# Attention with a top-32 mask and a gated product on one core: where GpSimd's difference of g, x's rounding and the copies of scores stand in their queues

## The chip, the cores and the metric

The kernel runs on one core of a Trainium2 chip. The time is the device time of one execution in microseconds, as the median of several runs. The engines of the core are TensorE (PE, with its weight loads PEld), VectorE (DVE), ScalarE (ACT), GpSimd (POOL) and SyncE (SP, which issues the DMAs). Each works through its own queue in order and waits on semaphores of the others.

## What is computed

For 8 batches and 8 heads of 576 rows and 64 columns, each row of scores keeps its 32 largest, goes through a softmax and multiplies v. The joined heads (4608 x 512) then go through three products:

```python
scores = scale * np.matmul(q, k.transpose(0, 1, 3, 2))
kth = np.partition(scores, -32, axis=-1)[..., -32:-31]
scores = np.where(scores >= kth, scores, -1e9)
attn = softmax(scores)
x = np.matmul(attn, v).transpose(0, 2, 1, 3).reshape(B * S, H * D)
out = ((x @ w1) * (x @ w2)) @ w3 @ w_out
```

## The kernel before

The attention is cut into 144 slots. A slot is 128 rows of two heads, 128 x 2 x 576 scores, found at lines 31 to 34 and listed at line 461. Twelve slots give 384 rows of x, one MoE block (`BLOCK`, line 38). w3 and w_out are multiplied together once at the start, into `wf`. To keep the precision of 32-bit numbers in rounded matmuls, x, g and the weights are each held as a rounded part and the difference to it, and a product takes three matmuls.

The main loop (line 568) has one step `p` per slot, and works on several slots at different stages at once: i = p + 1 has its scores copied from PSUM to SBUF, slot p is searched for its 32 largest, j = p - 1 is masked and goes through the exponential, l = p - 2 is normalised, and m = p - 3 is turned (transposed) and multiplied with v. All engines keep the order in which the program issues (`InOrder`, line 50), so where a line stands in the loop is where its instruction stands in the engine's queue.

In one step, the names and lines that matter here:

- ACT: `take_scores` (248) copies the scores of slot i in two parts: part 0 are columns 0 to 383 out of a bank pair called wide, part 1 columns 384 to 575 out of the tile `rest`. Even and odd slots have different wide banks (wide0, wide1) and share `rest` (`scores_whole`, 228). Then come the Relus of `mask` (295), evictions of MoE results, the copies of the turned weights (`take_turned`, 339), `normalise`, and the exponentials (`exps`). At the end of the loop body `split_high` (367) rounds x.
- DVE: `top32_steps` (255) folds the 576 columns in four instructions (`w<-s` twice, `w<-w,s` twice) and then takes four rounds of eight maxima with replacements between. `split_low` (370) follows the fold and takes the difference of x, `invert` the reciprocal, and `take_b` (377) the product of a and b.
- POOL: `edges_of` (272) makes `edge` (and `over`) from the maxima, `add_up` the sums, `mask` subtracts the Relu twice (`pab<-s,pab`; the first waits for the fold of the next slot), and `take_b` the difference of g.
- PE: `turn` (321) makes ten transposes, one of them into `rest`, eight into wide0, in each step. In even steps the scores of two slots and the values (`values`, 345) of two slots follow.

The MoE block is a generator (`moe_steps`, 373) that issues one matmul at each call, and `fill` (494) takes 12 of them at fixed places: one group of 12 in an even step, three in an odd one (`SHARES`, 46). A block begins in an odd step: 16 groups of 12 for a and b, two per f, then 8 groups for the four outputs. What follows a full group is put off until the next `evict`: a copy of a to `asb` on ACT (`take_a`), or `take_b`: the product with b on DVE, the rounding to g on ACT, and the difference on POOL. The outputs need rounded part and difference of all eight g.

`asb` and the output tile `osb` share two buffers; g has eight.

Of the kernel before, what the change touches and what calls it, by code (L numbers as in the profile page):

```python
# [9 lines left out]
F32 = mybir.dt.float32  # L10
# [4 lines left out]
ALU = mybir.AluOpType  # L15
# [55 lines left out]
def attn_moe(ctx: ExitStack, tc: tile.TileContext, q, k, v, w1, w2, w3, w_out, out, flag, any_missed, general):  # L71
    nc = tc.nc
    pe, act, dve, pool, sp = nc.tensor, nc.scalar, nc.vector, nc.gpsimd, nc.sync
# [37 lines left out]
    if not general:  # L111
        pe, act, dve, pool, sp = (InOrder(tc, e) for e in (pe, act, dve, pool, sp))
# [132 lines left out]
    def new_s():  # L245
        return att_p.tile([128, 2, S], F32, tag="s", name="s", bufs=S_BUFS)

    def take_scores(s, st, h):
        if isinstance(st[h], tuple):
            src, lo, hi = st[h]  # L250
        else:
            src, (lo, hi) = st[h][:, :, :HS], HALVES[h]
        act.copy(s[:, :, lo:hi], src)
# [41 lines left out]
    def mask(s, edge, pab, a, after=None):  # L295
        act.activation(pab[:, a, :], s[:, a, :], AF.Relu, bias=edge[:, a, 1:2], scale=-STEEP)
        ins = pool.tensor_tensor(pab[:, a, :], s[:, a, :], pab[:, a, :], op=ALU.subtract)
        if after is not None:
            tc.add_manual_dep(
                ins.ins, after.ins.name, mybir.DependencyInfo(mybir.DependencyClass.Sync, mybir.DependencyReason.DATA),  # L300
                reason="the fold of the next slot goes before the masking",
            )
# [64 lines left out]
    def split_high(high, low, whole):  # L367
        act.copy(high, whole)

    def split_low(high, low, whole):  # L370
        dve.tensor_tensor(low, whole, high.bitcast(F32), op=ALU.subtract)

    def moe_steps(xs, nb, places, after):
        def take_a(p, asb):
            act.copy(asb[:, :nb], p[:, :nb])

        def take_b(p, asb, gf):
            whole = asb[:, :nb]
            dve.tensor_tensor(whole, p[:, :nb], whole, op=ALU.mult)
            act.copy(gf[:, 0, :nb], whole)  # L380
            pool.tensor_tensor(gf[:, 1, :nb], whole, gf[:, 0, :nb].bitcast(F32), op=ALU.subtract)

        def take_o(p, e):
            osb = o_p.tile([128, NB], F32, tag="o", name="osb")
            act.copy(osb[:, :nb], p[:, :nb])
            for place, cut in places:
                sp.dma_start(place(slice(e * 128, (e + 1) * 128)), osb[:, cut])

        g = []
        for f in range(NFC):  # L390
            asb = o_p.tile([128, NB], F32, tag="o", name="asb")
            g.append(late["g"].tile([128, 2, NB], F32R, tag="g", name="g"))
            for i in range(2):
                p = late["mm"].tile([128, 512], F32, tag="mm", name="ab")
                for c in range(NCC):
                    for n, (w, x) in enumerate(((wh, 0), (wh, 1), (wl, 0))):
                        pe.matmul(
                            p[:, :nb], w[i][:, c * DF + f * 128 : c * DF + (f + 1) * 128], xs[c][:, x, :nb],
                            start=(c == 0 and n == 0), stop=(c == NCC - 1 and n == 2),
                        )  # L400
                        if (c, n) != (NCC - 1, 2):
                            yield
                if i == 0:
                    after(lambda p=p, asb=asb: take_a(p, asb))
                else:
                    after(lambda p=p, asb=asb, gf=g[f]: take_b(p, asb, gf))
                yield
        for e in range(NEC):
            p = late["mm"].tile([128, 512], F32, tag="mm", name="eo")
            for f in range(NFC):  # L410
                for n, (i, j) in enumerate(((0, 0), (1, 0), (0, 1))):
                    pe.matmul(
                        p[:, :nb], wf[i][:, f * DM + e * 128 : f * DM + (e + 1) * 128], g[f][:, j, :nb],
                        start=(f == 0 and n == 0), stop=(f == NFC - 1 and n == 2),
                    )
                    if (f, n) != (NFC - 1, 2):
                        yield
            after(lambda p=p, e=e: take_o(p, e))
            yield
# [82 lines left out]
    def begin():  # L502
        while starting:
            while going or fetched or waiting:
                warm()
            if not late:
                settle()
            n = starting.pop(0)
            queue.append(moe_steps([xs[n, hp] for hp in range(NHP)], NB, places[n], put_off.append))
# [24 lines left out]
    def warm():  # L534
        entered.append(p)
        if p < 0:
            return
        if fetched and len(entered) % 2 == 0:
            z, step = fetched.pop(0)
            going.append(step(z))  # L540
        going[:] = [unit for unit in going if next(unit, "end") != "end"]
        prefetch(WAITING)
# [20 lines left out]
    def scored(h):  # L563
        renew(kts, load_k, h)
        if h + 1 == n_slots or group_of[h + 1] != group_of[h]:
            renew_q(group_of[h] + 2)

    for p in range(-2, n_slots + 4):
        h, i, j, l, m = p + 2, p + 1, p - 1, p - 2, p - 3
        if p == 1:  # L570
            vts[0, 0] = load_v(0, 0)
            vts[0, 1] = load_v(0, 1)
            vts[0, 2] = load_v(0, 2)
            vts[0, 3] = load_v(0, 3)
        finder = top32_steps(ss[p], p) if 0 <= p < n_slots else iter(())
        if 0 <= i < n_slots:
            ss[i] = new_s()
            take_scores(ss[i], sts[i], 0)
            take_scores(ss[i], sts[i], 1)
        if 0 <= j < n_slots:  # L580
            edges[j] = edges_of(j)
        if 0 <= l < n_slots:
            add_up(pabs[l][1])
        folded = next(finder, None)
        for part in fresh:
            split_low(*part)
        fresh.clear()
        warm()
        if 0 <= j < n_slots:
            pabs[j] = new_weights()  # L590
            for a in range(2):
                mask(ss[j], edges[j], pabs[j][0], a, folded if a == 0 else None)
        warm()
        begin()
        fill(SHARES[p % 2][0])
        evict()
        next(finder, None)
        if 0 <= m < n_slots:
            turned[m] = take_turned(pabs[m][0], *turn(pabs[m][0], None if ("wide", 0) in late else sts[i][1]))
        if 0 <= l < n_slots:  # L600
            invert(pabs[l][1])
            normalise(*pabs[l])
        if 0 <= j < n_slots:
            exps(edges[j], *pabs[j], 0)
        warm()
        if p == 3:
            stir(6)
        fill(SHARES[p % 2][1])
        next(finder, None)
        warm()  # L610
        if h not in sts and (not late or h % 2) and h < n_slots:
            score(h, scores)
            scored(h)
        elif h % 2 == 0:
            for n in (h + 1, h):
                if n < n_slots:
                    score(n, lambda *a, n=n: scores_whole(*a, n % 2))
            for n in (h, h + 1):
                if n < n_slots:
                    scored(n)  # L620
            homes[:] = [wide_banks(1)[:, a, SPLIT:] for a in range(2)]
        if 0 <= j < n_slots:
            exps(edges[j], *pabs[j], 1)
        if 0 <= m < n_slots:
            if not put_back(m):
                for n in [m - 1, m] if put_back(m - 1) else [m]:
                    b, hps, t = slots[n]
                    ovs[n] = values(of(vts, b), hps, *turned.pop(n), n < m)
                    renew(vts, load_v, n)
        if p == 14:  # L630
            stir(9)
        next(finder, None)
        warm()
        fill(SHARES[p % 2][2])
        for _ in finder:
            pass
        for d in sorted(ovs):
            b, hps, t = slots[d]
            n = d // BLOCK
            for hp in hps:  # L640
                if (n, hp) not in xs:
                    xs[n, hp] = new_x(n)
            fresh += parts_of([xs[n, hp] for hp in hps], column[group_of[d]], t, ovs.pop(d))
            del ss[d], pabs[d], edges[d], sts[d]
            if (d + 1) % BLOCK == 0:
                starting.append(n)
        for part in fresh:
            split_high(*part)
        if p == 2:
            stir(8)  # L650
        warm()
    begin()
    worst = small.tile([128, B + 1], F32, tag="worst", name="worst", bufs=1)
    dve.tensor_reduce(worst[:, 1:], over[:].rearrange("p (b i) -> p b i", b=B), axis=AX.X, op=ALU.max)
# [65 lines left out]
```

## Time and profile before

| | us |
|---|---|
| time, median of 3 runs (1315.67 to 1315.72) | 1315.68 |
| the profiled execution, its own time | 1318.25 |
| its span, first to last instruction | 1316.5 |
| DVE busy | 1192.0 |
| PE busy | 1197.6 |
| ACT busy | 1112.7 |
| POOL busy | 777.4 |

The first 190 us bring in and unpack the weights beside the first slots; from there to about 1235 us the steady part runs; the last 50 us are the last MoE block, on PE almost alone. In the rows below a line of the timeline gives the start and the length in us, the engine, the instruction with the tile that it writes and those that it reads, and in brackets the idle time of the engine before it and what ended it. Instructions that follow at once are merged (x2). The ends of matmuls are modelled.

### The profile page before, as it was taken

The numbers are of one execution on the slowest core, as the hardware profiler recorded it, in microseconds if no ns is written. First come the engines' busy times: TensorE is split into PE (matmuls) and PEld (weight loads), VectorE is DVE, ScalarE is ACT, GpSimd is POOL, SyncE is SP. The second block draws the span as 40 slices with busy tenths as digits, with TensorE's granted clock in tenths as the row PEclk, the third lists the DMA queues.
The fourth block names the chain that finished last, engine by engine and source line by source line (L and its number), as shares of the span: only waits on it lengthen the run. The fifth ranks groups of instructions, "written<-read, shape, count | busy, mean of one in ns | idle before, by whom it ended". The sixth has DMA issues, their size and how long they took to land.

```text
span 1316.5 us, 27368 instructions
## 1 busy us (share of the span) xinstructions
PE 1197.6 (91%) x9427; PEld 1039.0 (79%) x9427; DVE 1192.0 (91%) x3952; ACT 1112.7 (85%) x2233; POOL 777.4 (59%) x877
## 2 busy tenths in 40 slices
PE   5788689999999999999999999999999999999998
PEld 3444368888888888888888888888888888888998
DVE  7999999999999999999999999999999999999710
ACT  5988989989989989989989989989989989889821
POOL 4778766656656656656656656656656656656511
PEclk6899899999999999999999999999999999999999
DMA  7334210100120020101120020101120020100000
GB/s 283 113 120 153 96 57 9 60 27 30 35 71 9 16 75 9 60 28 30 35 71 9 15 75 9 60 28 31 34 70 10 15 76 9 60 27 1 13 13 26
DMA packets 30117, 64.73 MB, mean 49 GB/s; under 512 B 5396, under 2 KB 11540, under 8 KB 29972
## 3 DMA queue, kind: packets, MB, share of 16 engines
q1 hardware_dynamic: 29972, 62.93, 14.7%
q8 instruction: 75, 1.23, 0.4%
q14 instruction: 70, 0.57, 0.1%
HBM read 53.48 MB, written 9.44 MB: 48 GB/s over the span
## 4 chain that ended last, share of the span: by engine, by line
PE 49%; ACT 26%; DVE 14%; issue 6%; POOL 4%; DMA 1%; SPq 0%; ACTq 0%; POOLq 0%; DVEq 0%
PE wide L60 22%; ACT pab L60 18%; PE ab L60 14%; PE eo L60 7%; DVE w L60 5%; PE rest L60 5%; ACT s L60 5%; DVE top L60 5%; POOL pab L60 2%; DVE t L60 1%; POOL g L60 1%; ACT g L60 1%; DVE x L60 1%; DMA z<-in_wo 1%; ACT x L60 1%
## 5 line engine op out<-in xcount | busy, mean ns | idle before, releaser
L60 POOL TENSOR_TENSOR pab<-s,pab 128x576 f32<-128x576 f32 x288 | 404.8, 1428 | 145.9 <-PE ab L60 49.2
L60 DVE MAX8 top<-w 128x8 f32<-128x192 f32 (+1 forms) x1152 | 465.7, 445 | 0.0
L60 PE MATMUL ab<-x,wh 128*128 128x384 f32 x1536 | 408.0, 347 | 0.6 <-ACT asb L60 0.5
L60 DVE MATCH_REPLACE8 w<-top,w 128x192 f32<-128x192 f32 x864 | 289.3, 342 | 0.0
L60 PEld LDWEIGHTS ab<-x,wh 128*128 128x128 f32 x1536 | 271.1, 188 | 8.7 <-issue 7.3
L60 PE MATMUL ab<-x,wl 128*128 128x384 f32 x768 | 259.7, 338 | 0.0
L60 POOL TENSOR_TENSOR g<-asb,g 128x384 fp32r<-128x384 f32 x96 | 105.5, 1099 | 252.9 <-ACT g L60 252.9
L60 ACT ACTIVATE pab<-s,edge 128x576 f32<-128x576 f32 x288 | 210.5, 789 | 37.4 <-POOL edge L60 37.4
L60 ACT ACTIVATE pab<-pab,edge 128x576 f32<-128x576 f32 x288 | 220.6, 774 | 1.2 <-POOL pab L60 1.2
L60 PE MATMUL eo<-g,wf 128*128 128x384 f32 x1152 | 220.0, 344 | 0.0
L60 ACT ACTIVATE pab<-pab,sums 128x576 f32<-128x576 f32 x288 | 209.7, 785 | 10.2 <-DVE sums L60 10.2
L60 DVE TENSOR_TENSOR w<-s 128x384 f32<-128x384 f32 x288 | 193.2, 711 | 14.8 <-ACT s L60 7.6
L60 PEld LDWEIGHTS eo<-g,wf 128*128 128x128 f32 x1152 | 199.8, 188 | 3.4 <-issue 3.1
L60 DVE TENSOR_TENSOR w<-w,s 128x384 f32<-128x384 f32 x288 | 168.3, 584 | 4.9
L60 PE MATMUL wide<-pab,vt 128*64 128x128 f32 (+1 forms) x2960 | 160.1, 264 | 0.6 <-ACT pab L60 0.6
L60 PEld LDWEIGHTS wide<-pab,vt 128*64 128x64 f32 x2960 | 144.7, 137 | 16.1 <-issue 15.3
L60 PE MATMUL wide<-ident,pab 128*128 128x128 f32 x1040 | 152.2, 272 | 0.0
L60 ACT COPY pab<-wide 128x1024 f32<-128x1024 f32 x130 | 132.1, 1016 | 17.6 <-PE wide L60 12.9
L60 PEld LDWEIGHTS ab<-x,wl 128*128 128x128 f32 x768 | 144.2, 188 | 0.0
L60 PEld LDWEIGHTS wide<-ident,pab 128*128 128x128 f32 x1040 | 125.6, 140 | 4.5
L60 POOL TENSOR_TENSOR edge<-top,coef 128x4 f32<-128x4 f32 x144 | 72.8, 505 | 67.3 <-DVE top L60 67.2
L60 PE MATMUL wide<-kt,qt 64*128 64x384 f32 (+1 forms) x560 | 108.6, 506 | 0.7 <-ACT pab L60 0.7
(64 smaller groups left out, 1394.9 us busy)
## 6 DMA issues: line engine op xcount, KB each, us to landing
z<-in_w SPq DMA_DIRECT2D x32, 512.0 KB, 3.6
vt<-in_v SPq DMA_DIRECT2D x32, 352.0 KB, 4.4
qt<-in_q SPq DMA_DIRECT2D x40, 256.0 KB, 2.8
kt<-in_k SPq DMA_DIRECT2D x32, 320.0 KB, 3.4
out_t<-osb SPq DMA_DIRECT2D x32, 192.0 KB, 1.9
z<-in_wo SPq DMA_DIRECT2D x8, 512.0 KB, 8.2
out_t<-osb SPq DMA_DIRECT2D x16, 160.0 KB, 1.8
out_t<-osb SPq DMA_DIRECT2D x16, 32.0 KB, 1.6
```

Source lines behind the costliest of these rows:

```text
L60: ins = fn(*args, **kw)
```

## The change

Three things are put elsewhere; no instruction is added or taken away. POOL's difference of g is no longer issued in `take_b` but kept in a list, and issued in the main loop behind the masks of the next step. ACT copies part 1 of the scores (from `rest`) ahead of part 0. The rounding of x moves from the end of the loop body to the next step, behind its copies of scores.

```diff
+    lows, behind_masks = [], []
+
+    def take_lows():
+        while lows:
+            lows.pop(0)()
+
     def moe_steps(xs, nb, places, after):
...
-            pool.tensor_tensor(gf[:, 1, :nb], whole, gf[:, 0, :nb].bitcast(F32), op=ALU.subtract)
+            lows.append(lambda: pool.tensor_tensor(gf[:, 1, :nb], whole, gf[:, 0, :nb].bitcast(F32), op=ALU.subtract))
+            if not behind_masks:
+                take_lows()
...
+    behind_masks.append(True)
     for p in range(-2, n_slots + 4):
...
             ss[i] = new_s()
+            take_scores(ss[i], sts[i], 1)
             take_scores(ss[i], sts[i], 0)
-            take_scores(ss[i], sts[i], 1)
+        for part in fresh:
+            split_high(*part)
         if 0 <= j < n_slots:
             edges[j] = edges_of(j)
...
                 mask(ss[j], edges[j], pabs[j][0], a, folded if a == 0 else None)
+        take_lows()
         warm()
         begin()
...
-        for part in fresh:
-            split_high(*part)
         if p == 2:
             stir(8)
         warm()
+    take_lows()
+    behind_masks.clear()
     begin()
```

## Rows read from the trace of the kernel before

**Rows 1.** The page, part 1: busy us, share of the span, instructions.
```profile
PE 1197.6 (91%) x9427; PEld 1039.0 (79%) x9427; DVE 1192.0 (91%) x3952; ACT 1112.7 (85%) x2233; POOL 777.4 (59%) x877
```

**Rows 2.** One block: busy PE, PEld, DVE, ACT, POOL; granted clock, DMA share, GB/s.
```profile
587.38:685.79 98.41, 92.52 (x732) 82.99 (x732) 94.80 (x321) 87.42 (x176) 59.01 (x69) 1.00 0.16 45
```

**Rows 3.** Waits, whole span: us in total, times, longest.
```profile
PE rest L60 <- ACT s L60: 61.5, 63, 1.2
```

**Rows 4.** The chain that ended last, two of its pieces in the steady part.
```profile
602.91 1.08 ACT s L60 x2
...
604.04 0.33 PE rest L60
```

**Rows 5.** Timeline of PE.
```profile
548.63 3.60 PE L60 MATMUL eo<-g,wf 128*128 128x384 f32 x19
...
571.06 0.33 PE L60 MATMUL rest<-ident,pab 128*128 128x128 f32 x1 [1.24 <-ACT s L60]
...
604.04 0.33 PE L60 MATMUL rest<-ident,pab 128*128 128x128 f32 x1 [0.98 <-ACT s L60]
...
620.61 0.33 PE L60 MATMUL rest<-ident,pab 128*128 128x128 f32 x1 [0.98 <-ACT s L60]
```

**Rows 6.** Timeline of ACT.
```profile
578.47 0.43 ACT L60 CAST x<-wide 128x128 fp32r<-128x128 f32 x2 [1.84 <-PE wide L60]
...
602.41 0.50 ACT L60 CAST g<-asb 128x384 fp32r<-128x384 f32 x1
602.81 0.80 ACT L60 COPY s<-wide 128x768 f32<-128x768 f32 x1
603.50 0.48 ACT L60 COPY s<-rest 128x384 f32<-128x384 f32 x1
604.82 1.45 ACT L60 ACTIVATE pab<-s,edge 128x576 f32<-128x576 f32 x2 [0.83 <-POOL edge L60]
...
611.70 0.43 ACT L60 CAST x<-wide 128x128 fp32r<-128x128 f32 x2 [0.75 <-PE wide L60]
...
615.04 1.02 ACT L60 COPY pab<-wide 128x1024 f32<-128x1024 f32 x1
...
618.97 0.50 ACT L60 CAST g<-asb 128x384 fp32r<-128x384 f32 x1
```

**Rows 7.** Groups of instructions by form, whole span: count, busy us, mean ns.
```profile
L60 DVE TENSOR_TENSOR w<-s 128x384 f32<-128x384 f32 x288 | 193.2, 711 | 14.8 <-ACT s L60 7.6
L60 POOL TENSOR_TENSOR g<-asb,g 128x384 fp32r<-128x384 f32 x96 | 105.5, 1099 | 252.9 <-ACT g L60 252.9
```

**Rows 8.** Timeline of DVE.
```profile
560.34 1.03 DVE L60 TENSOR_TENSOR w<-s 128x384 f32<-128x384 f32 x2
...
601.45 1.41 DVE L60 MAX8 top<-w 128x8 f32<-128x576 f32 x2
602.89 1.83 DVE L60 TENSOR_TENSOR w<-s 128x384 f32<-128x384 f32 x2
...
606.29 0.34 DVE L60 MATCH_REPLACE8 w<-top,w 128x192 f32<-128x192 f32 x1
...
609.03 0.34 DVE L60 MATCH_REPLACE8 w<-top,w 128x192 f32<-128x192 f32 x1
```

**Rows 9.** Timeline of POOL.
```profile
548.02 2.82 POOL L60 TENSOR_TENSOR pab<-s,pab 128x576 f32<-128x576 f32 x2 [0.86 <-ACT pab L60]
...
602.99 1.32 POOL L60 TENSOR_TENSOR g<-asb,g 128x384 fp32r<-128x384 f32 x1 [2.76 <-ACT g L60]
604.27 0.51 POOL L60 TENSOR_TENSOR edge<-top,coef 128x4 f32<-128x4 f32 x1
...
605.96 2.80 POOL L60 TENSOR_TENSOR pab<-s,pab 128x576 f32<-128x576 f32 x2
```

**Rows 10.** The chain in the start, two pieces one step apart.
```profile
93.15 2.20 ACT pab L60 x4
...
105.67 2.20 ACT pab L60 x4
```

## Prediction

> **What bounds the kernel now.** I read the page first: PE and DVE are each busy 91% of the span, ACT 85%, POOL 59% [rows 1]. No engine is full, so shares decide nothing and I went to the steady part. Work repeats every two steps (an even one that scores and multiplies by v for two slots, an odd one that does neither) and every six such pairs (one MoE block). One block lasts 98.4 us at the full granted clock (1.00, the 2.4 GHz level), of which DVE is busy 94.8, PE 92.5 and ACT 87.4 [rows 2]. Next the waits: PE waits 63 times, 61.5 us in all, for a copy of scores by ACT before the transpose that goes into the shared bank `rest`; once per even step, 0.98 us each [rows 3]. Then the chain: in the steady part it runs PE's transpose into `rest`, the 12 MoE matmuls, the scores, the 40 value matmuls, ACT's rounding of x, ACT's odd step, g's rounding, two copies of scores, and the same transpose again [rows 4]. DVE appears there only for short stretches.
>
> One pair in numbers, from the two transposes into `rest` at 604.04 and 620.61 [rows 5]: 7.66 us until ACT rounds x at 611.70, 3.34 until ACT may copy the turned weights at 615.04 (that is PE's odd group and its turning, not ACT), 3.93 of ACT work to g's rounding at 618.97, and 1.64 for g's rounding, both score copies and the hand-over [rows 5, 6]. Sum 16.57. This loop is the bound.
>
> **Part 1, the shared bank's scores first.** In an even step ACT rounds g at 602.41, copies the wide scores at 602.81 and the `rest` scores at 603.50; the latter ends at 603.98 and PE's transpose goes at 604.04 [rows 5, 6]. So PE follows the `rest` copy by 0.06 us. With it first, it starts at 602.81 and PE goes 0.69 us (603.50 - 602.81) earlier. ACT's own work stays the same, and the wide copy then lies beside PE's transposes, whose bank (wide0) it doesn't read in an even step (it reads wide1, needed again only by the scores over 2 us later). Of PE's 0.98 us wait 0.29 is left, so PE doesn't become the limit before the whole 0.69 is taken. 63 waits x 0.69 = **43.5 us**. In odd steps nobody waits for the order. The fold on DVE reads scores copied one step before, so it doesn't notice.
>
> **Part 2, x's rounding behind the copies.** Today it stands ahead of the odd step's score copies, where ACT waits 0.75 us for the values with 1.06 us of copies (0.69 and 0.37) queued behind [rows 6]. After the edit the copies fill that wait. But ACT's turned copy at 615.04 waits for PE anyway, so this shortens nothing in the loop: x, the two Relus and a's copy take 0.33 + 1.34 + 0.36 = 2.0 us of the 3.34. The gain is slack, and odd masks that can start earlier. Its price is an x up to 0.2 us later, hidden by the same slack. DVE's difference of x comes behind its fold in any case, and the first MoE group of a new block needs x only in its later matmuls. Taken as 0, bounds -0.3 to +0.3 per block.
>
> **Part 3, g's difference behind the masks.** It removes no instruction: 96 subtractions of 1.10 us [rows 7] move past edge, over, sums and both masks. Two effects.
> First, DVE. With a g subtraction beside it the first half of the fold takes 1.83 us (602.89, subtraction at 602.99); in steps without one it takes 1.03 (560.34) [rows 8, 9]. The mean over all 288 instructions is 0.711 against 0.515 in the free step: 288 x 0.196 = 56 us, some 5 us of DVE per block [rows 7, 8]. So DVE's need falls from 94.8 to about 90. This is needed: at the shorter block of 93.7 to 94 us 94.8 wouldn't fit.
> The Trainium skill has a rule that speaks against the new place: SBUF — State Buffer, section "SBUF: two separate sides", says that a VectorE instruction with two SBUF inputs and a GpSimd instruction that reads SBUF lock each other out whole. By it the replacements behind the masks, which read both `w` and `top`, could be caught. The trace does not show that: a replacement takes 0.34 us beside the masks (606.29) and 0.34 after them (609.03) [rows 8]. Were they caught, it would be the first rival below, with the price that stands there.
> Second, the edge. It stands behind the subtraction on POOL: at 604.27 though top was ready at 602.86, so the Relus wait 0.83 us [rows 6, 8, 9]. In such pairs the copy of the turned rest comes late and PE's scores wait: 7.66 us from transpose to x instead of 7.41 (571.06 to 578.47) [rows 5, 6]. I count two such pairs per block, 0.25 to 0.33 each. Without the subtraction ahead, edge would be ready by 602.86 + 0.05 + 0.51 = 603.4, before the Relu can follow the copies at about 603.9 [rows 6, 8, 9]. 0.6 x 10.5 blocks = **6 us**.
>
> The wait it adds: the subtraction waits for nothing new (g's rounding is done), and behind it on POOL is only the next edge, some 2 us later. What waits for it is PE: the twelfth matmul of the second output group of a block reads the last g's difference. That group starts at 548.63 with 0.18 us per matmul, so its last goes at about 550.7; the masks of that step run 548.02 to 550.84 and the moved subtraction would end at 551.8 [rows 5, 9]. The masks waited 0.86 us for ACT's Relus there [rows 9], which come earlier after part 2; of that I count half, 0.4, because the fold holds the masks too. So PE waits about 0.7, of which 0.29 lies in what is left of its wait for ACT. Bounds 0 and 1.1 per block; I take 0.3: 11 x 0.3 = **3 us** lost. The buffers of a and of g, two and eight deep, come free a whole step before they are needed.
>
> **Start and end.** In the first 190 us a step takes 12.5 us in a loop of DVE and ACT (normalising at 93.15, 105.67) in which score copies don't stand [rows 10]. x's rounding changes places with the copies there at equal sum. Bounds -1 and +2 us, taken +0.5. The tail is PE's last MoE block, with the subtraction at once as before. Queues of DMAs issue what they did; no load moves past another.
>
> **Sum.** -43.5 - 6 + 3 + 0.5 = -46. The profiled execution has a span of 1316.5 and a time of 1318.25; the median of the runs is 1315.68, so I take the 46 from the median: **1269.5 us**. A block should take 93.8 instead of 98.4.
>
> **Rivals.**
> *DVE becomes the bound.* The subtraction finds DVE in the new place too, or the fold stays slow beside other POOL work. With no relief DVE needs 94.8 per block and more for its waits, 95.5; with every subtraction costing it a full microsecond (8 per block) 90 + 8 = 98. Saved are then 0.4 to 2.9 us of each of 10.5 blocks: 1285 to 1311, about 1297 in the middle. Against it: masks of 2.8 us already lie beside the same DVE work without lengthening it [rows 8, 9].
> *PE's transpose waits for both copies.* The row names ACT and s, not which copy. Then only the edge's 6 us come: about 1310; where the edge gives nothing either, 1315, no change. Against it: the start is 0.06 us behind the `rest` copy's end and 0.43 behind the wide copy's [rows 5, 6].
> *The last difference of g is late,* the one that would end slower. If POOL's masks slip at the start of the outputs, PE stands in its queue with everything behind it. Each microsecond beyond 0.29 costs 11 us; the gain of 49 is gone at 4.7 us. At 6 us it gives 1266 + 11 x 5.7 = 1329. Against it: the masks before that group waited 0.86 [rows 9].
> *More than forecast.* If the wait of PE goes entirely, because something ahead in ACT's chain shrinks too: 61.5 + 6 off, 1248. Against it: each piece of ACT's 3.93 us stays.
>
> **How the numbers follow.** Forecast 0.72, own range 1260 to 1280 (the bounds of the small terms). DVE bound 0.13, both copies 0.07 (half of it no change), last difference 0.03, more than forecast 0.05. For 8 in 10 the range runs from 1258 to 1288, which takes in the forecast and the near side of the first rival. About 0.2% is what a measurement of this kernel can tell from none. Faster 0.72 + 0.13 + 0.05 + 0.035 = 0.93, within 0.04, slower 0.03.
>
> **What would show it.** Right: PE's wait for ACT's s falls to about 0.3 us, 63 times (about 20 us in all); the distance of transposes into `rest` falls to about 15.6 us; the fold's first half takes 1.03 us in all steps and DVE's mean for it falls to near 0.52; the wait of ACT for edge is nearly gone; POOL's g stands behind pab. Wrong: PE's wait names another ACT row at equal length, or DVE shows no idle time, or PE's `eo` waits for POOL's g by more than a microsecond.

## The result and the profile after

The changed kernel takes 1271.55 us (median of 4 runs, 1270.52 to 1272.72), the kernel before 1315.70 on the same chip (1315.67 to 1317.92): a ratio of 0.9661, 95% interval 0.9644 to 0.9677, 44 us less. The profiled execution took 1270.52 us at a span of 1268.7, against 1318.25 and 1316.5 before.

The page, part 1, of the kernel after (busy us, share of the span, instructions), to be read against [rows 1]:

```profile
PE 1194.6 (94%) x9427; PEld 1036.4 (82%) x9427; DVE 1142.0 (90%) x3952; ACT 1108.1 (87%) x2233; POOL 769.8 (61%) x877
```

Every engine has the instructions it had. DVE is busy 50 us less, nearly all of it the fold (below); PE's and ACT's work is what it was, in a shorter span.

Two blocks of the kernel after by the table of windows (length; busy PE, PEld, DVE, ACT, POOL; granted clock, DMA share, GB/s); the second has the instruction counts of [rows 2]:

```profile
474.97:568.93 93.96, 92.56 (x828) 82.99 (x829) 90.56 (x325) 87.24 (x181) 58.30 (x69) 1.00 0.10 33
568.93:662.62 93.69, 92.17 (x732) 82.78 (x732) 90.28 (x321) 86.98 (x177) 58.28 (x69) 1.00 0.16 48
```

A block takes 93.69 us instead of 98.41, and DVE's work in it 90.28 instead of 94.80. The clock is the full one in both. Some 10.5 blocks of 4.7 us make 49 us, about the 47.8 by which the two spans differ.

The waits of the kernel after (total us, times, longest), over the whole span, which answer to [rows 3]:

```profile
PE rest L60 <- ACT s L60: 14.5, 53, 0.3
...
PEld eo L60 <- POOL g L60: 7.1, 11, 2.6
PE eo L60 <- POOL g L60: 3.4, 7, 2.3
```

PE's wait for the copies of scores has gone from 61.5 to 14.5 us. The wait of the outputs (`eo`) for the last difference of g is new, as the prediction feared, and small in all; but one of the seven waits of PE is 2.3 us long, and a wait of more than a microsecond there was one of the prediction's signs of being wrong. It is taken up below, at the run that issues the last g at once.

The chain that ended last in the kernel after, across one hand-over (start, length, what), against [rows 4], where two copies stood in one piece:

```profile
489.74 0.40 ACT g L60
490.14 0.38 ACT s L60
...
490.57 0.33 PE rest L60
```

One pair on the timeline of PE, of ACT and of POOL, as in [rows 5, 6, 9] (start and length in us, engine, instruction, idle time before it and its cause):

```profile
490.57 0.33 PE L60 MATMUL rest<-ident,pab 128*128 128x128 f32 x1 [0.28 <-ACT s L60]
...
506.21 0.33 PE L60 MATMUL rest<-ident,pab 128*128 128x128 f32 x1 [0.28 <-ACT s L60]
```
```profile
490.05 0.47 ACT L60 COPY s<-rest 128x384 f32<-128x384 f32 x1
490.42 0.80 ACT L60 COPY s<-wide 128x768 f32<-128x768 f32 x1
491.11 1.46 ACT L60 ACTIVATE pab<-s,edge 128x576 f32<-128x576 f32 x2
...
501.35 1.01 ACT L60 COPY pab<-wide 128x1024 f32<-128x1024 f32 x1 [0.56 <-PE wide L60]
...
505.28 0.50 ACT L60 CAST g<-asb 128x384 fp32r<-128x384 f32 x1
```
```profile
489.88 0.50 POOL L60 TENSOR_TENSOR edge<-top,coef 128x4 f32<-128x4 f32 x1 [2.18 <-DVE top L60]
...
492.03 2.81 POOL L60 TENSOR_TENSOR pab<-s,pab 128x576 f32<-128x576 f32 x2 [0.69 <-ACT pab L60]
494.79 1.01 POOL L60 TENSOR_TENSOR g<-asb,g 128x384 fp32r<-128x384 f32 x1
```

The distance of the two transposes into `rest` is 15.64 us instead of 16.57. From the transpose to the turned copy it is 10.78 (501.35 - 490.57) instead of 11.00 (`edge` is no longer late), then 3.93 of ACT's work as before (g's rounding follows at 505.28), and 0.93 instead of 1.64 to the next transpose (the order of the copies). `edge` starts at 489.88, ahead of the copies, and is ready before the Relus, which follow the copies without a gap. The subtraction of g stands behind the masks and takes 1.01 us.

Groups of the kernel after by form (count, busy us and mean ns of one, idle time before them and its cause), against [rows 7]:

```profile
L60 DVE TENSOR_TENSOR w<-s 128x384 f32<-128x384 f32 x288 | 148.5, 557 | 13.3 <-ACT s L60 7.4
L60 POOL TENSOR_TENSOR g<-asb,g 128x384 fp32r<-128x384 f32 x96 | 97.5, 1015 | 42.2 <-ACT g L60 42.2
L60 ACT ACTIVATE pab<-s,edge 128x576 f32<-128x576 f32 x288 | 211.7, 798 | 7.4 <-POOL edge L60 7.3
```

The first half of the fold has fallen from 711 to 557 ns, 45 us in all (busy 193.2 to 148.5), its second half by another 9 (168.3 to 159.4), and the Relus' wait for `edge` is 7 us in all.

### The profile page after: what moved, and what is told of

Same layout as the page of the kernel before. It is cut to its first block, busy times and chain, and to the rows that moved or that the text cites. A ratio compares the mean times of both kernels' runs of the same rounds, so it can differ in the third digit from the quotient of the medians.

```text
span 1268.7 us, 27365 instructions
## 1 busy us (share of the span) xinstructions
PE 1194.6 (94%) x9427; PEld 1036.4 (82%) x9427; DVE 1142.0 (90%) x3952; ACT 1108.1 (87%) x2233; POOL 769.8 (61%) x877
## 4 chain that ended last, share of the span: by engine, by line
PE 49%; DVE 22%; ACT 21%; issue 4%; POOL 3%; ACTq 0%; POOLq 0%; DVEq 0%
PE wide L60 20%; PE ab L60 15%; ACT pab L60 15%; DVE w L60 10%; PE eo L60 8%; DVE top L60 8%; PE rest L60 4%; ACT s L60 2%; POOL pab L60 2%; DVE t L60 2%; ACT g L60 1%; DVE x L60 1%; DVE z L60 1%; ACT x L60 1%; POOL g L60 1%
## 5 line engine op out<-in xcount | busy, mean ns | idle before, releaser
L60 POOL TENSOR_TENSOR pab<-s,pab 128x576 f32<-128x576 f32 x288 | 404.5, 1427 | 137.8 <-ACT pab L60 97.3
L60 PE MATMUL eo<-g,wf 128*128 128x384 f32 x1152 | 223.2, 345 | 3.6 <-POOL g L60 3.4
L60 PEld LDWEIGHTS eo<-g,wf 128*128 128x128 f32 x1152 | 199.3, 188 | 10.5 <-POOL g L60 7.1
L60 DVE TENSOR_TENSOR w<-w,s 128x384 f32<-128x384 f32 x288 | 159.4, 553 | 4.9
L60 DVE TENSOR_TENSOR w<-s 128x384 f32<-128x384 f32 x288 | 148.5, 557 | 13.3 <-ACT s L60 7.4
L60 POOL TENSOR_TENSOR g<-asb,g 128x384 fp32r<-128x384 f32 x96 | 97.5, 1015 | 42.2 <-ACT g L60 42.2
```

The source lines that it names most:

```text
L60: ins = fn(*args, **kw)
```

## The experiments

The theory that the prediction rests on has three terms that are added: 43.5 us from the order of the copies (part 1), 0 from x (part 2), 3 to 6 from g's subtraction (part 3). The first four runs take the parts singly, and parts 1 and 3 together, with the kernel before beside them at 1317.16 us.

### Part 1 alone

```diff
             ss[i] = new_s()
+            take_scores(ss[i], sts[i], 1)
             take_scores(ss[i], sts[i], 0)
-            take_scores(ss[i], sts[i], 1)
```

> Part 1 alone: the scores of `rest` are copied first, x and g stand where they stood. Theory (the loop of PE and ACT is the bound, and DVE is close behind it while g's difference lies beside the fold): PE's wait before its transpose into `rest` falls, but DVE needs 94.8 us of each block, so a block falls only from 98.4 to about 95.5 to 96.5 and the time to 1285 to 1297; the fold's first half stays at 1.7 to 1.8 us in steps with g. Rival (the copies' order alone carries the gain): about 1272, as with all three parts.

Measured: 1303.12 us (1302.13 to 1305.98), ratio 0.9896 (0.9879 to 0.9913). That is 14 us gained, below both expectations. The waits of PE in it, from 190 us to 1235:

```profile
PE rest L60 <- ACT pab L60: 23.3, 42, 0.8
PE rest L60 <- ACT s L60: 17.3, 63, 0.5
```

The wait for the copies of scores has fallen as forecast, 61.5 to 17.3, but a wait has come up that PE's rows of the kernel before do not have (there only the weight loads wait so, 19.9 us; here they wait 50.0): 42 times PE's scores into `rest` wait for ACT's copy of the turned `rest`. One such place, on the timelines of POOL, ACT and PE:

```profile
499.00 1.40 POOL L60 TENSOR_TENSOR g<-asb,g 128x384 fp32r<-128x384 f32 x1 [2.73 <-DVE top L60]
500.37 0.51 POOL L60 TENSOR_TENSOR edge<-top,coef 128x4 f32<-128x4 f32 x1
```
```profile
500.91 1.45 ACT L60 ACTIVATE pab<-s,edge 128x576 f32<-128x576 f32 x2 [0.91 <-POOL edge L60]
```
```profile
482.73 0.33 PE L60 MATMUL rest<-ident,pab 128*128 128x128 f32 x1 [0.28 <-ACT s L60]
...
499.35 0.33 PE L60 MATMUL rest<-ident,pab 128*128 128x128 f32 x1 [0.28 <-ACT s L60]
...
503.85 0.60 PE L60 MATMUL rest<-kt,qt 64*128 64x192 f32 x4 [0.77 <-ACT pab L60]
```

PE saves 0.70 us at the transpose and stands 0.77 at the scores, 4 us later. ACT has its copies done but waits 0.91 for `edge`, which stands on POOL behind the subtraction of g; the Relus are late, with them the copy of the turned rest, with that PE. The pair 482.73 to 499.35 takes 16.62 us, no less than before. Part 1's 0.69 is there, but the late `edge` takes it back, in four pairs of each six. The two pairs of a block with output groups keep it (15.6 us instead of 16.3): 21 of them x 0.69 are the 14 us.

### Part 2 alone

```diff
             take_scores(ss[i], sts[i], 1)
+        for part in fresh:
+            split_high(*part)
...
-        for part in fresh:
-            split_high(*part)
```

> Part 2 alone: x's rounding behind the copies of scores. Theory: it only makes slack on ACT, whose next copy waits for PE in the odd step anyway: 1312 to 1317. Rival (ACT's odd step is a bound): each pair is shorter by up to 0.75 us, 63 times, so down to 1270.

Measured: 1317.71 us, ratio 1.0 (0.999 to 1.0009). Nothing, as forecast.

### Part 3 alone

The change's lines on `lows`, without the other two parts:

```diff
+            lows.append(lambda: pool.tensor_tensor(gf[:, 1, :nb], whole, gf[:, 0, :nb].bitcast(F32), op=ALU.subtract))
...
                 mask(ss[j], edges[j], pabs[j][0], a, folded if a == 0 else None)
+        take_lows()
```

> Part 3 alone: g's difference behind the masks. Theory: DVE is not the bound before, so its 5 us per block give nothing by themselves; what comes is the edge's 6 us less the late last g: 1309 to 1313, PE still waits 0.98 us for the `rest` copy in each even step, and the fold's first half takes 1.03 us everywhere. Rival (DVE's contention was the bound): the time falls by most of the 44 us, to 1275 to 1285.

Measured: 1311.69 us, ratio 0.9962 (0.9948 to 0.9976), 5.5 us gained. The first half of the fold takes 557 ns here too and DVE is busy 1142.6 us, 49 less, yet the time hardly moves: PE still waits for both copies (longest 1.2 us). Relieving DVE is worth little by itself while the loop of [rows 5, 6] is the bound. By the rows the 5.5 us are the edge's: the Relus' wait for it falls from 37.4 to 6.7 us, and the two pairs of a block that took 16.6 us take 16.3; but the run shortens the fold with the same edit, so this is read and not separated. The late last g costs next to nothing here: the outputs wait for it 11 times, 11.2 us in all, but PE waits for the copies ten times less (53).

### Parts 1 and 3, without x

```diff
-        for part in fresh:
-            split_high(*part)
         if 0 <= j < n_slots:
...
+        for part in fresh:
+            split_high(*part)
         if p == 2:
```

(against the kernel after)

> Parts 1 and 3 without part 2. Theory: x's place is free of cost, so 1269 to 1276, the time of all three. Rival: with x ahead of the copies the odd step of ACT (x, two copies, two Relus, a's copy: 3.1 us) leaves so little of the 3.34 us before PE's turn that the masks or ACT's turned copy come late: 1280 to 1290.

Measured: 1279.43 us, ratio 0.9709 (0.9692 to 0.9725), between the two expectations. The pairs with a and b groups are as short as in the kernel after (15.64). What is lost is lost where the outputs begin. ACT, POOL and PE there:

```profile
531.90 0.56 ACT L60 CAST x<-wide 128x64 fp32r<-128x64 f32 x4 [0.90 <-PE wide L60]
...
533.39 1.49 ACT L60 ACTIVATE pab<-s,edge 128x576 f32<-128x576 f32 x2
```
```profile
534.30 2.82 POOL L60 TENSOR_TENSOR pab<-s,pab 128x576 f32<-128x576 f32 x2 [1.72 <-ACT pab L60]
537.09 1.00 POOL L60 TENSOR_TENSOR g<-asb,g 128x384 fp32r<-128x384 f32 x1
```
```profile
538.14 2.56 PE L60 MATMUL eo<-g,wf 128*128 128x384 f32 x13 [1.05 <-POOL g L60]
```

The same place in the kernel after, POOL and PE:

```profile
530.97 2.81 POOL L60 TENSOR_TENSOR pab<-s,pab 128x576 f32<-128x576 f32 x2 [0.70 <-ACT pab L60]
533.74 1.01 POOL L60 TENSOR_TENSOR g<-asb,g 128x384 fp32r<-128x384 f32 x1
```
```profile
532.58 4.79 PE L60 MATMUL eo<-g,wf 128*128 128x384 f32 x24
```

With x ahead of the copies ACT stands 0.90 us for the values with the copies and the Relus behind it. POOL's masks wait 1.72 us for the Relus instead of 0.70, the subtraction behind them is a microsecond later, and PE stands 1.05 us in the second output group, where in the kernel after the 24 matmuls run through. Over the whole run PE's row of `eo` waiting for POOL's g is 12.0 us in 11 waits against 3.4 in 7: 8.6 us, and the two kernels differ by 8. So part 2, worth nothing alone, is worth 8 us beside parts 1 and 3. Parts 2 and 3 without part 1 were not run.

### Parts 1 and 2, without g

```diff
             ss[i] = new_s()
+            take_scores(ss[i], sts[i], 1)
             take_scores(ss[i], sts[i], 0)
-            take_scores(ss[i], sts[i], 1)
+        for part in fresh:
+            split_high(*part)
```

> Parts 1 and 2 without part 3. What the first four runs showed: part 1 alone gives 14 us, because in the pairs with a and b PE's scores wait for the copy of the turned rest, which waits for the Relus, which wait for edge, which stands behind g's difference. Theory: x's place changes nothing in that, so 1300 to 1305, as part 1 alone. Rival: part 2 gives its 8 us of the full change here too: 1293 to 1297.

Measured: 1302.88 us, ratio 0.9887 (0.9872 to 0.9902), as part 1 alone. So part 3 is worth 5.5 us alone and 31 beside the others. Two reasons are possible, the late `edge` and the longer fold, for DVE is nearly full in this kernel as well. A block of it by the table of windows:

```profile
483.84:581.06 97.22, 93.28 (x828) 83.06 (x829) 95.07 (x325) 88.01 (x181) 59.09 (x69) 1.00 0.10 32
```

DVE is busy 95.07 of 97.22 us, and its waits in the block are two, 0.9 and 0.3 us. The next two runs were made to part the reasons.

### A late edge with a short fold

On the kernel after: three fills of the tile of differences, which wait for g's rounding (`cast`) and come ahead of `edge` on POOL, stand where the subtraction stood. The subtraction, behind the masks, overwrites them.

```diff
-            act.copy(gf[:, 0, :nb], whole)
+            cast = act.copy(gf[:, 0, :nb], whole)
+            for _ in range(3 if behind_masks else 0):
+                ins = pool.memset(gf[:, 1, :nb].bitcast(F32), 0.0)
...
```

> The changed kernel with its g difference behind the masks, and three fills of 128x384 on POOL where the difference stood before (each waits for g's rounding, writes and reads nothing; together about 1.2 us, as the difference took). This makes edge late without putting an instruction that reads two tiles beside DVE's fold. Theory A (edge's place on POOL is what gave part 1's gain back): edge late by 0.9 us in four pairs of a block, PE's scores wait some 0.7 us more in each: 1295 to 1305, while the fold stays at 1.03 us. Theory B (DVE's longer fold gave it back): 1271 to 1276. If the fills lengthen the fold too, the run doesn't tell them apart.

Measured: 1309.40 us (1308.74 to 1310.7), ratio 0.9941 (0.9924 to 0.9957). A block of it by windows, its waits of PE (190 to 1235 us), its fold and its Relus by form, and one place on POOL:

```profile
485.15:582.47 97.32, 93.35 (x829) 83.05 (x829) 90.94 (x325) 88.03 (x181) 61.88 (x93) 1.00 0.10 32
```
```profile
PE rest L60 <- ACT pab L60: 24.3, 42, 0.6
...
PE eo L60 <- POOL g L60: 6.4, 11, 3.1
```
```profile
L60 ACT ACTIVATE pab<-s,edge 128x576 f32<-128x576 f32 x288 | 208.6, 775 | 47.0 <-POOL edge L60 46.2
L60 DVE TENSOR_TENSOR w<-s 128x384 f32<-128x384 f32 x288 | 148.7, 557 | 13.5 <-ACT s L60 7.7
```
```profile
501.20 1.37 POOL L60 MEMSET g<- 128x384 f32 x3 [2.27 <-ACT g L60]
502.54 0.37 POOL L60 TENSOR_TENSOR edge<-top,coef 128x4 f32<-128x4 f32 x1
```

The fold is as short as in the kernel after (557 ns), DVE is not busy for 6.4 us of the block, and still the block is 97.3 us and PE has the same 42 waits for ACT's copy as with part 1 alone. Its pairs with a and b groups take 16.4 to 16.7 us; with parts 1 and 2 alone it is 16.2 to 16.7, in the kernel after 15.6 to 15.8. A late `edge` suffices to give part 1's gain back. The time is above the expected range, and 6.5 us above parts 1 and 2 alone. The Relus' wait for `edge` doesn't explain that, for it is as long there (45.5 us). Some 2 us of it lie in the 61 pairs from 210 to 1200 us (988.7 against 986.5), the rest behind them, where the outputs of the eleventh block wait 3.1 us for g, a wait that parts 1 and 2 alone don't have.

### A long fold with an early edge

On the kernel after: the subtraction goes behind `edge`, `over` and the sums, ahead of the masks, so that it would meet the fold.

```diff
         if 0 <= l < n_slots:
             add_up(pabs[l][1])
+        take_lows()
...
-        take_lows()
         warm()
```

> The changed kernel, but g's difference goes directly behind edge, over and sums, ahead of the masks. This tells two reasons apart why part 1 needs part 3. If it is the place of edge in POOL's queue, edge is early here too and the time stays at 1271 to 1278. If it is DVE's need (the difference still lies beside the fold, which takes 1.7 us in its first half, or its second), DVE needs 94.8 us per block and the time is 1285 to 1303. I expect the second, since edge itself depends on DVE's maxima, and DVE would fall behind by about 0.3 us per pair until edge is late again.

Measured: 1268.45 us, ratio 0.9627 (0.9612 to 0.9641), where 1285 to 1303 was expected. The fold and the subtraction, by form and at one place (POOL, DVE):

```profile
L60 DVE TENSOR_TENSOR w<-s 128x384 f32<-128x384 f32 x288 | 148.5, 557 | 13.2 <-ACT s L60 7.4
L60 POOL TENSOR_TENSOR g<-asb,g 128x384 fp32r<-128x384 f32 x96 | 124.3, 1295 | 47.3 <-ACT g L60 40.2
```
```profile
508.19 1.32 POOL L60 TENSOR_TENSOR g<-asb,g 128x384 fp32r<-128x384 f32 x1
```
```profile
507.49 1.14 DVE L60 TENSOR_TENSOR w<-w,s 128x384 f32<-128x384 f32 x2
508.54 0.61 DVE L60 MAX8 top<-w 128x8 f32<-128x192 f32 x2
```

The run did not do what it was made for: the two meet, but now POOL pays (1295 ns instead of 1015) and the fold is as short as without it. So it doesn't tell what a long fold alone would cost, and that stays open. With `edge` early and the fold short, as in the kernel after, it doesn't part the two reasons either; that is left to the run with the fills. It does show that the place behind the masks is not the only good one: with the subtraction earlier the outputs don't wait for it (no such row for PE), and the time is some 3 us lower.

### The last g at once; the transpose into rest last

What is left in the kernel after are the outputs' wait for g and the 0.28 us of PE. Two edits on the kernel after take one each (`last` is f == NFC - 1; the transpose `te` goes behind the loop over the other eight; there are nine in all, not ten), and a third kernel has both; the kernel after runs beside them at 1270.94 (ratio 0.9649), the kernel before at 1317.71.

```diff
-            if not behind_masks:
+            if last or not behind_masks:
                 take_lows()
```

> The changed kernel, but the difference of the last g of each block is issued at once, as before the change, so that PE's second output group doesn't wait for it. Theory: PE waits for it 7.1 us at its weight loads in 11 blocks, part of it covered by its next wait for ACT: 2 to 5 us faster than the changed kernel. Rival: what is taken there returns in the fold (one fold of 1.8 instead of 1.0 us per block) or in the wait for ACT: no difference within 1 us.

Measured: 1268.71 us, ratio 0.9628 (0.9615 to 0.9641), 2.2 us below the kernel after. PE's rows no longer show a wait for g; one fold per block is long again (mean 588 ns). The gain isn't spread over the blocks: the 61 pairs from 209 to 1163 us take 953.8 us, in the kernel after 953.7. Six of the seven waits there are 0.2 us and cost nothing; the seventh, in the eleventh block at the end of the attention, is what is won:

```profile
1191.32 2.57 PE L60 MATMUL eo<-g,wf 128*128 128x384 f32 x13 [2.32 <-POOL g L60]
```

The run with the subtraction behind `edge`, also without that wait, has the same 61 pairs (953.8 us), so its 3 us don't lie in them either.

```diff
-            if a == 0:
-                pe.transpose(te, flat[:, 512:640], ident)
+        pe.transpose(te, flat[:, 512:640], ident)
```

> The changed kernel, with PE's transpose into `rest` behind the other eight instead of between them. PE then has 0.33 us of transposes to do while it waits for the `rest` copy, of which 0.28 are left. Theory (the loop of PE and ACT through that transpose is still the bound): a pair falls from 15.63 to about 15.3 us and the time by up to 63 x 0.3 = 19 us, to 1252 to 1260, unless DVE (15.6 us in the pairs with a and b, 14.6 in the others) takes over, then 1260 to 1266. Rival (the remaining wait costs nothing): 1270 to 1273.

Measured: 1267.18 us, ratio 0.9619 (0.9606 to 0.9632), 3.8 us below the kernel after, where 11 or more were expected, or 5 at least if DVE took over. PE's wait at the transpose is gone, and there is another in its place, on the timeline of PE:

```profile
488.59 0.33 PE L60 MATMUL rest<-ident,pab 128*128 128x128 f32 x1
...
492.08 0.59 PE L60 MATMUL rest<-kt,qt 64*128 64x192 f32 x4 [0.19 <-ACT pab L60]
...
504.23 0.33 PE L60 MATMUL rest<-ident,pab 128*128 128x128 f32 x1
```

The pair with a and b groups is 15.64 us long, as without the edit: the next tie, the copy of the turned rest, is there at once, now with no late `edge` behind it, only ACT's own work. The gain comes from the two pairs of a block with output groups, 15.1 and 15.2 us instead of 15.5 and 15.6. Part of it is lost in the pair in which the outputs begin, which takes 16.1 us instead of 15.7.

> The last g at once and the transpose into `rest` last. Theory: the gains add up where DVE leaves room: 1250 to 1262. Rival: DVE is the bound by then, and the time is that of the better of the two alone.

Measured, both together: 1261.93 us (1260.73 to 1262.17), ratio 0.9577 (0.9564 to 0.9591), 9 us below the kernel after. That is more than 2.2 and 3.8 together: with the last g at once the pair in which the outputs begin is no longer than in the kernel after, and the pairs with output groups keep their 15.2.

### Both wide scores ahead of both rest scores

On the kernel with both edits: PE makes the wide scores of two slots (`which` 0) and then the `rest` scores of both (1), so that the `rest` scores start 4.06 us behind the transpose instead of 3.49.

```diff
-            for n in (h + 1, h):
-                if n < n_slots:
-                    score(n, lambda *a, n=n: scores_whole(*a, n % 2))
+            for which in (0, 1):
+                for n in (h + 1, h):
+                    if n < n_slots:
+                        score(n, lambda *a, n=n: scores_whole(*a, n % 2, which))
```

> The last g at once and the transpose into `rest` last, and in addition PE computes both wide parts of the scores ahead of both parts in `rest`, so that it no longer waits (0.19 us, 42 times) for the copy of the turned rest. Theory A (that copy is the loop that binds after the transposes' order): pairs with a and b fall from 15.64 to about 15.4 us, the time by 8 to 12 us, to 1250 to 1254. Theory B (DVE binds there: its steps of 7.51 and 8.13 us add up to 15.64, the pair itself): no more than 2 us, 1260 to 1262.

Measured: 1256.09 us (1255.07 to 1256.5), ratio 0.9532 (0.9519 to 0.9545), between the two expectations and 15 us below the kernel after: the best version here. One block by windows, and DVE's folds one pair apart:

```profile
487.02:579.73 92.71, 92.61 (x814) 83.22 (x812) 91.13 (x325) 87.14 (x181) 58.52 (x69) 1.00 0.10 34
```
```profile
486.21 1.03 DVE L60 TENSOR_TENSOR w<-s 128x384 f32<-128x384 f32 x2
...
501.67 1.03 DVE L60 TENSOR_TENSOR w<-s 128x384 f32<-128x384 f32 x2
```

PE has no wait for ACT's copies left in the block, and DVE has one of 0.6 us. DVE's instructions follow each other almost without a gap over the 15.46 us of a pair, and PE, too, is busy 92.61 of the 92.71 us, with modelled ends. That from here on only less work on DVE, or on PE, would help is a reading of these rows and was not tried.

## Why the prediction was right, step by step

**The bound and part 1.** The loop through PE's transpose, and the place where the order of the copies ends it, were read rightly: PE's wait is 0.28 us where 0.29 was forecast, the pair 15.64 where 15.6 was. But the sum treats the 43.5 us as part 1's own. Part 1 alone brought 14: the step that was missing is the next tie in the loop, the scores that wait for the copy of the turned rest, which waits for `edge` behind g's subtraction. The row for it stood in the prediction, the Relus' wait of 0.83 us [rows 6], and was priced at 0.3 us in two pairs of a block, which is right only while the transpose itself is late. The chain of the kernel before showed the tie as well, one pair ahead of the one that was worked out:

```profile
586.33 1.42 POOL g L60
587.74 0.48 POOL edge L60
```

**Part 3.** The 6 us alone were 5.5. The fold's first half is 1.03 us in every step of the steady part and DVE's work in a block 90.3 us, where about 90 was forecast. But the 56 us behind that were misread: 711 ns is the mean of single instructions, whose ends overlap, and 515 is half of a merged pair. By busy time the row lost 45 us, and its mean fell to 557, not to the 520 that was named as a sign; the fold's second half made up for it. That the relief is "needed" is right as arithmetic, for 94.8 us of DVE's work don't fit into a block of 93.7. It is the smaller reason: the run with the late `edge` loses 3.5 of the 4.6 us of a block (97.3 against 93.8) with DVE relieved. What a long fold alone would cost was not measured; an estimate from DVE's busy time is at least 94.8 - 93.7 = 1.1 us a block, some 12 us. Part 3 also did what the sum didn't give it, 31 us beside parts 1 and 2 instead of 6; the sum comes out right because the total of parts 1 and 3 was counted once, under part 1.

**Part 2.** "Taken as 0" is right alone and beside part 1 (1302.88 against 1303.12) and wrong beside parts 1 and 3: 8 us, or 0.7 per block, outside the bounds of 0.3. The mechanism was in the prediction (the Relus "come earlier after part 2", of which it counted half), but in the term for the last g, as something given.

**The last g.** Forecast 3 us lost, 0.3 in each of 11 blocks; issuing that one at once wins 2.2 back. The size is right and the place is not: the blocks lose nothing, and one wait of 2.3 us at the end of the attention is the whole of it.

**Replacements behind the masks.** They were not caught: 343 ns in the mean over 864, 342 before. The trace has a load of eight values of its own ahead of each (864, 77 ns), so a replacement may not have had the two inputs that the prediction gave it. The first rival did not occur; had part 3 not relieved the loop, the time would have been 1303, within that rival's 1285 to 1311.

**Start and sum.** The first transpose of the steady part stands at 209.22 us against 209.77 before, so the start cost nothing (forecast 0.5). A block takes 93.7 to 94.0 (forecast 93.8), the time is 1271.55 (forecast 1269.5), 44 us less instead of 46. That it comes so close is in part luck: parts 1 and 3 without part 2 bring 38 us (1317.16 to 1279.43) where their terms give 46, and part 2, taken as 0, adds the rest.

## What to carry to other kernels

When a wait is taken out of a loop between engines, look for the next wait in the same loop and for what would make it late: here some 30 of 44 us hung on a 128x4 instruction queued behind a big one on another engine. Moves that measure nothing alone can be worth much together, so try them in pairs before dropping one. Put the small instruction that others wait for ahead of the large one that nobody needs yet.

## What was not expected of the hardware

The meeting of DVE's fold and POOL's subtraction costs whichever comes second, instruction by instruction. In the kernel before, the fold began at 602.89 and the subtraction at 602.99, which took 1.32 us instead of the 1.01 it takes free, and the fold's second instruction came after it (1.83 us for two instead of 1.03) [rows 8, 9]. With the subtraction behind `edge` it met the last fold instruction, took 1.32 us again, and DVE lost nothing, since the maxima that follow on DVE were not held up (0.61 us, as without it). The Trainium skill (SBUF — State Buffer, "SBUF: two separate sides") says that the first to start keeps the shared port for its whole instruction; both traces agree. The replacements showed no such wait in any run here; whether they have two inputs, after the load of eight values ahead of each, no run here shows.

Fills on POOL, which only write, left the fold at 557 ns in the run that has three of them ahead of `edge`; the Trainium skill's rule, which speaks of GpSimd instructions that read, agrees.
